# Two layers of linear attention and MLP on one core: the order of a pair's seven products, and the slots of the work beside them

## The chip, the core and the metric

The kernel runs on one core of a Trainium2 chip. The metric is the device time of one execution in microseconds (us), from launch to end; the profile also has a span, from the first to the last instruction, which is a little shorter. A core has five engines that run side by side and wait for one another by semaphores: TensorE (PE in the profile; PEld is its loading of weights) multiplies matrices, VectorE (DVE) and ScalarE (ACT) do elementwise work, GpSimd (POOL) too, and SyncE (SP) issues nearly all transfers (DMA). Each engine takes its own instructions strictly in the order in which the program issues them.

## The reference

The input x has 2048 rows (tokens) of 448 float32 numbers. Two layers with the same weights follow one another; each adds linear attention and then an MLP:

```python
phi = lambda t: jnp.where(t > 0, t + 1, jnp.exp(t)) + 1e-6
# attention, 16 heads of 28
q, k, v = split(x @ wqkv)
kv, z = einsum("bhsd,bhse->bhde", phi(k), v), einsum("bhsd->bhd", phi(k))
o = (phi(q) @ kv) / (phi(q) @ z + 1e-6)
return o @ wo
# MLP, 448 -> 1792 -> 448
return gelu(x @ w1 + b1) @ w2 + b2
# the whole
for _ in range(2):
    x = x + A(layernorm(x))
    x = x + B(layernorm(x))
```

## The kernel before

All matrix operands are kept as two numbers, a rounded high part and the rest as a low part, and a product of two such matrices is made as three: high by high, high by low, low by high. Splitting an operand therefore takes a copy on ACT (the high part) and a subtraction on DVE or POOL (the low part), and PE waits for both.

The 2048 tokens are 16 tiles of 128 rows. A layer has these stages:

**Phase 1** (`phase1`, line 797; steps by the strings `STEPS` and `STEP`) goes over the tiles: LayerNorm (`stage_a`, statistics, line 521; `stage_n`, normalising, line 524), turning the tile for PE (`stage_t`, `turn`), splitting it (`stage_x`, line 551, with the DVE subtraction of line 365), the products for k and q (psk and psq, line 382), phi, the low part of phi(k) (kl, line 611), and the sum G of phi(k) by x (`stage_g`, line 724). The turning goes by way of memory: DVE transposes blocks of 32, SP stores the square (`store_sq`) and loads it back spread (`spread`).

**Attention of the first query group and the end of phase 1** is an order written out by hand, the string `ORDER` (line 733), one token for each step. Its token `pre` loads the four phi(q) tiles of the second group (`load_pq`, lines 938 to 941) and starts the loading of a piece of w1 (`make`, line 484, with `raw`, lines 419 and 420, for the transfer).

**The MLP** treats four groups of 512 tokens. For groups 0 and 1, `classic` (line 1320) runs 14 steps each: `mlp1` multiplies by one chunk of w1 (11 matmuls of 512 columns, line 1199) and applies gelu, `mlp2` multiplies the previous chunk's gelu output by a chunk of w2 (12 matmuls of 448 columns, lines 1229 to 1231) into four accumulators. Beside them, step i does what string i of `PLAN` (line 1247) lists for the attention of groups 1 to 3: `z` and `p` (denominators, scaling, turning of phi(q): lines 951 and 962 to 973 and `turn`), `sq` and `lq` (store and load of the turned squares), `q` (splitting, ql on line 365), `o` (product with the output matrix, lines 1021 to 1025, and LayerNorm statistics), `n` (normalising), `sx`, `lx`, `x` (the same for the MLP's input). The first digit of a token is the group, the second the tile in it.

For groups 2 and 3 together, `eight` (line 1376) makes the first product by seven products instead of eight (a Strassen scheme over two chunks of w1 and the two groups) for each of seven pairs k of chunks. Products 1, 5, 6 and 7 are six matmuls of 512 columns, products 2, 3 and 4 five (line 1141). They accumulate in three banks: X takes products 1, 6, 7 and 4, Y takes 5 and 3, Z takes 2. Between them the partial sums are saved or added (`keep`, a copy on ACT, line 1145; s1, s2 and s5 with DVE adds), gelu and the split of its result follow (`high`: gelu and high part on ACT; `low`: the low part gl on DVE, line 1176), and two of the four results are stored for group 3 (`later`). `mlp2` for group 2 takes two chunks per pair, of which 2k-1 is the previous pair's second result and 2k this pair's first. Pair 0 also holds the last two chunks of group 1, whose results leave the accumulators by four DVE adds (r, line 1234), and the last piece A22 of the input (`token_piece`, line 1108, DVE subtraction on line 1112).

The seven weight combinations of the next pair are made in ten steps by a generator (`sevens`, line 445), one of which runs at every call of `step()` or `make`: the transfer (`raw`), a split with ACT line 429 and POOL lines 430 and 431, a DVE copy on line 457 that reads what line 430 wrote, POOL differences, and so on, to the last one with ACT line 478 and DVE line 479. `beside` (line 1354) loads residual rows (`back`) and, in layer 0, loads and splits wk and wq and loads x for the next layer.

**Rest** (`rest`, line 1453) loads group 3's stored gelu outputs back, splits them (`divide`) and multiplies them by w2, 14 chunks. In layer 0 the string `REST` (line 1451) puts beside it the start of layer 1: `a` statistics, `n` normalising and turning, `s` store, `p` load, `x` splitting, `m` weights. Before it, `table(AF.Exp)` loads ACT's table for exp.

The two orders that the change replaces, in short (M is a call of `mlp2`, the numbers are products, for k of 1 and more):

```
before:  1 5 M(2k-1) 6 2 7 3 4 M(2k)
after:   1 5 2 6 M(2k-1) 3 7 M(2k) 4
```

Of the kernel before, what the change touches and what calls it, by code (L numbers as in the profile page):

```python
# [11 lines left out]
AF = mybir.ActivationFunctionType  # L12
# [10 lines left out]
def linear_attn_mlp_kernel(  # L23
# [176 lines left out]
    def table(func):  # L200

        act.activation(none, tiny, func)
# [281 lines left out]
    def make(n, steps=1):  # L484
        if n < len(ahead):
            if n not in makers:
                makers[n] = (sevens if ahead[n][1] == "x" else chunks)(n)
            for _ in range(steps):
                next(makers[n], None)
# [220 lines left out]
    def stage_g(l, t, acc, mid=lambda: None):  # L710
# [22 lines left out]
    ORDER = [  # L733
# [3 lines left out]
    ] * LAYERS  # L737
    DEFER = NT - sum(tok in ("Q", "Qa", "Qy") for tok in ORDER[0].split())

# [30 lines left out]
    def load_to(l, t):  # L770
        for u in range(loaded.get(l, 0), t + 1):
            load_x(l, u)
        loaded[l] = max(loaded.get(l, 0), t + 1)
# [23 lines left out]
    def phase1(l, tr):  # L797
        za = consts.tile([128, D], F32, name="za", tag="za")
        acc = []
        load_to(l, 4 if l == 0 else NORM[l][1][-1])  # L800
        if l == 0:
            launch(za)
            load_to(l, NORM[l][2][-1])
        for t in range(l == 0, NT):
            norm = NORM[l][t] if t < len(NORM[l]) else ()
            for tok in STEPS.get((l, t), STEP).split():
                if tok[1:].isdigit() and tok[0] in "anv":
                    {"a": stage_a, "n": stage_n, "v": stage_t}[tok[0]](l, int(tok[1:]))
                elif tok == "q1":
                    stage_qphi(1)  # L810
                elif tok == "sp":
                    for key, h in list(stored):
                        block(key)
                        spread(key, h)
                elif tok == "ld" and t + 2 < len(NORM[l]):
                    load_to(l, NORM[l][t + 2][-1])
                elif tok == "a":
                    for u in norm:
                        stage_a(l, u)
                elif tok == "n":  # L820
                    for u in norm:
                        stage_n(l, u)
                elif tok == "tu":
                    for u in norm:
                        stage_t(l, u)
                elif tok == "T" and t + 1 < NT:
                    stage_b(l, t + 1, "acc" if t == 1 else "h")
                elif tok == "X" and t + 1 < NT and (l == 0 or t + 1 >= 4):
                    stage_x(l, t + 1)
                elif tok == "K":  # L830
                    stage_k(l, t)
                elif tok == "qp":
                    stage_qphi()
                elif tok == "kp":
                    stage_kphi(l, t)
                elif tok == "kh":
                    stage_kh(l, t)
                    if l == 0:
                        begin(BG[t])
                elif tok == "kl":  # L840
                    stage_kl(l, t, za)
                elif tok == "s":
                    stage_s(l, t)
                elif tok == "G" and t >= 1:
                    acc = acc or [bank("acc", 4, f"G{c}")[:, :D] for c in range(4)]
                    stage_g(l, t - 1, acc)
                elif tok == "bg" and l == 0:
                    background(BG[t - 1])
                elif tok == "Q" and t < DEFER:
                    stage_q(l, t)  # L850
            if t == 12:
                tr.wv = stage_square(wqkv[:, 2 * D:])
            if t == 13:
                trans_load(l, tr)
        return za, acc
# [252 lines left out]
    def token_piece(l, name, h, eng=dve):  # L1108
        x = view(l, name, h)
        hi, lo = (cols(placed(l, k, name, h)) for k in range(2))  # L1110
        act.copy(hi, x)
        eng.tensor_tensor(lo, x, f(hi), op=OP.subtract)
# [91 lines left out]
    def mlp2(l, b, i, then=lambda: None):  # L1204
# [49 lines left out]
        "q12 o11 n10 p22 z23 ld30",  # L1254
        "q13 o12 n11 sx10 ld31",
        "o13 n12 lq20 p23 sq21 z30 ld32",
        "n13 lx10 sx11 p30 z31 g20 ld33",
        "x10 lq21 p31 sq30 z32 g21",
        "x11 lx11 q20 p32 z33 g22",
        "x12 x13 q21 o20 p33 sq31 g23",  # L1260
        "q22 o21 n20 lq30 g30",
        "q23 o22 n21 sx20 g31",
        "q30 o23 n22 lq31 g32 g33",
        "q31 o30 n23 sx21",
        "q32 o31 n30 r10 r11",
        "q33 o32 n31 sx30 lx21 r12 r13",
        "o33 n32 lx20 tA111 b10",
# [86 lines left out]
    def beside(l, k):  # L1354

        nonlocal st_k, st_q
        if 2 <= k < 6:
            back(l, 2, k - 2)
        if 3 <= k < 7:
            add_bias(l, 2, k - 3)  # L1360
        if k == 5:
            gb.load(l, 4)
        if l + 1 == LAYERS:
            return
        if k == 5:
            load_to(l + 1, PRE - 1)
        if k == 1:
            st_k = stage_square(wqkv[:, D:2 * D])
        if k == 2:
            split_kq("k", st_k)  # L1370
        if k == 3:
            st_q = stage_square(wqkv[:, :D])
        if k == 4:
            split_kq("q", st_q)

    def eight(l, k):

        n = first_pair(l, 2) + k
        c = Pair(l, k, n)

        def step():
            if k < NP - 1:
                make(n + 1)

        c.product(1)
        s1 = c.keep(c.X, "s1")
        if k == 0:
            mlp2(l, 1, NF - 2)
            c.product(2)
            dve.tensor_tensor(s1, s1, c.Z, op=OP.add)  # L1390
            token_piece(l, "A22", 0)
            c.high(s1, 0)
        step()
        c.product(5)
        s5 = c.keep(c.Y, "s5")
        step()
        if k:
            mlp2(l, 2, 2 * k - 1)
        c.product(6)
        s2 = c.keep(c.X, "s2")  # L1400
        make(n)
        if k == 0:
            c.low(0)
            token_piece(l, "A22", 1)
            mlp2(l, 1, NF - 1)
        if k < NP - 2:
            make(n + 2)
        step()
        if k:
            c.product(2)  # L1410
            dve.tensor_tensor(s1, s1, c.Z, op=OP.add)  # L1411
            c.high(s1, 0)
            step()
        c.product(7)
        dve.tensor_tensor(s5, c.X, s5, op=OP.add)
        if k:
            c.low(0)
        c.later(s5, 1)
        step()
        c.product(3)  # L1420
        dve.tensor_tensor(s2, s2, c.Y, op=OP.add)
        c.high(s2, 1)
        step()
        if k == 0:
            mlp2(l, 2, 0)
        c.product(4)
        c.low(1)
        c.later(c.X, 0)
        step()
        if k:  # L1430
            beside(l, k)
            mlp2(l, 2, 2 * k)
        step()

    class Came:

# [11 lines left out]

    gb = Came()

    REST = ("a0", "n0 a1", "n1", "a2 m0", "s0 n2 a3", "n3 m1", "m0", "s1 p0 a4", "n4 m0", "m1", "p1 x0", "x1 m1", "", "x2 x3")

    def rest(l):

        gb.load(l, 2)
        g = gb.x.pop(0)
        gs[0] = divide_high(g)
        mlp2(l, 2, NF - 1, lambda: divide_low(g, *gs[0]))
        for i in range(NF):
            if i + 1 < NF:  # L1460
                divide(i + 1, gb.x.pop(i + 1))
            gb.load(l)
            if 5 <= i < 9:
                back(l, 3, i - 5)
            if 8 <= i < 12:
                add_bias(l, 3, i - 8)
            if l + 1 < LAYERS:
                for tok in REST[i].split():
                    t = int(tok[1:])
                    if tok[0] == "a":  # L1470
                        stage_a(l + 1, t)
                    elif tok[0] == "n":
                        stage_n(l + 1, t)
                        turn(xns[l + 1, t], ("a", l + 1, t // 4), t % 4)
                    elif tok[0] == "s":
                        store_sq(("a", l + 1, 0), t)
                    elif tok[0] == "p":
                        stage_sp(l + 1, t * 2 + 1)
                    elif tok[0] == "x":
                        stage_x(l + 1, t)  # L1480
                    elif tok[0] == "m":
                        make(first_pair(l + 1, 0) + t)
            mlp2(l, 3, i)
        gb.n = 0
# [29 lines left out]
    for l in range(LAYERS):  # L1514
# [37 lines left out]
            classic(l, b, tr)  # L1552
        for k in range(NP):
            eight(l, k)
        if l + 1 < LAYERS:
            table(AF.Exp)
        rest(l)


# [26 lines left out]
```

## Time and profile before

| | us |
|---|---|
| median of 3 runs | 864.94 |
| lowest and highest of them | 862.77, 865.45 |
| the profiled execution, its own time | 862.32 |
| its span, first to last instruction | 860.7 |
| around the span in that execution | 1.6 |

PE is busy for 847.2 us of the span (98%), DVE 616.9, ACT 442.9, POOL 392.1. The granted clock of TensorE is 1.000 over the span.

How to read the rows that follow. A row of the timeline has the start in us from the span's start, the duration in us, engine, line of the kernel, operation, what is written and read, the shape, and how many instructions it merges; in brackets stands the idle time of the engine just before it and what ended that. A row of the waits has who waited for whom, the total in us, how often and the longest. A row of a window has, for each engine, the busy us and in brackets the number of instructions, then the granted clock, the share of the DMA engines and GB/s. A row of a group has count, busy us, mean ns of one, and idle time before. Matmuls are pipelined, so that a row's duration is longer than the distance to the next row.

### The profile page before, as it was taken

To read this page: it belongs to the slowest core of one execution; us is meant where nothing else is said; L and a number is where in the kernel's file an instruction comes from. 1 tells how busy PE (TensorE), PEld (TensorE's weight loads), DVE (VectorE), ACT (ScalarE), POOL (GpSimd) and SP (SyncE) were. 2 spreads that over 40 slices of the span, in tenths; PEclk is the share of its full clock that TensorE was granted. 3 is DMA by queue.
4 is the path that set the end of the run, shared out by engine and by line. 5 is a ranking of instruction groups with operands and counts; after the bars stand their busy time and mean duration, and the time that the engine had idled before them with its cause. 6 is when DMAs were issued, how large, how long until landed. Compare 5 with 4: busy or idle time off the path is not lost.

```text
span 860.7 us, 12463 instructions
## 1 busy us (share of the span) xinstructions
PE 847.2 (98%) x4085; PEld 753.4 (88%) x4085; DVE 616.9 (72%) x1094; ACT 442.9 (51%) x883; POOL 392.1 (46%) x460
## 2 busy tenths in 40 slices
PE   9999999999999999999999999999999999999998
PEld 8899988788888888888899998988888888788897
DVE  7899586799965765465879876868998657534343
ACT  7667665335334556574345665553343346556531
POOL 3456523547426744751633344144563367453320
PEclk9999999999999999999999999999999999999999
DMA  5375736758656033418635542476668540432271
GB/s 171 119 246 178 245 104 219 256 164 278 215 193 225 13 120 114 148 60 290 213 119 190 166 158 97 130 244 213 212 209 271 194 165 3 134 101 91 98 232 43
DMA packets 103636, 142.91 MB, mean 166 GB/s; under 512 B 9876, under 2 KB 90644, under 8 KB 103572
## 3 DMA queue, kind: packets, MB, share of 16 engines
q1 hardware_dynamic: 101156, 138.77, 49.1%
q10 hardware_dynamic: 2416, 3.36, 1.2%
q8 instruction: 32, 0.52, 0.3%
q14 instruction: 32, 0.26, 0.1%
HBM read 88.94 MB, written 49.02 MB: 160 GB/s over the span
## 4 chain that ended last, share of the span: by engine, by line
PE 67%; DVE 15%; DMA 5%; issue 5%; ACT 4%; POOL 3%; SPq 0%; ACTq 0%; DVEq 0%; POOLq 0%
PE hp L1199 7%; PE G L724 7%; PE psk L382 7%; PE y L1231 7%; PE psq L382 6%; PE y L1229 6%; PE y L1230 6%; PE hx L1141 6%; PE hy L1141 3%; DVE gl L1176 2%; DVE ql L365 2%; DMA pq<-pq_d 1%; DVE pq L973 1%; DMA sp<-sq_m 1%; PE hz L1141 1%
## 5 line engine op out<-in xcount | busy, mean ns | idle before, releaser
L1229 PE MATMUL y<-w2h,gh 128*128 128x448 f32 x447 | 162.6, 364 | 1.9 <-DVE r L1234 1.7
L1230 PE MATMUL y<-w2l,gh 128*128 128x448 f32 x447 | 163.6, 366 | 0.0
L1231 PE MATMUL y<-w2h,gl 128*128 128x448 f32 x447 | 161.2, 361 | 1.8 <-DVE gl L1176 1.8
L1176 DVE TENSOR_TENSOR gl<-g,gh 128x512 fp32r<-128x512 f32 x84 | 67.4, 802 | 89.3 <-ACT gh L1172 89.3
L1199 PE MATMUL hp<-XH,W 128*128 128x512 f32 x392 | 123.6, 389 | 0.9 <-POOL W L431 0.9
L1201 ACT ACTIVATE g<-hp,b1s 128x512 f32<-128x512 f32 x56 | 38.5, 688 | 150.6 <-PE hp L1199 150.0
L213 POOL TENSOR_TENSOR brs<-bve,few 128x1 f32<-128x1 f32 x55 | 36.0, 654 | 134.3 <-DVE bve L212 130.5
L1229 PEld LDWEIGHTS y<-w2h,gh 128*128 128x128 f32 x447 | 83.7, 187 | 12.4 <-DVE r L1234 2.8
L1231 PEld LDWEIGHTS y<-w2h,gl 128*128 128x128 f32 x447 | 84.0, 188 | 10.0 <-DVE gl L1176 4.7
L1230 PEld LDWEIGHTS y<-w2l,gh 128*128 128x128 f32 x447 | 83.9, 188 | 6.2
L1199 PEld LDWEIGHTS hp<-XH,W 128*128 128x128 f32 x392 | 73.6, 188 | 13.8 <-POOL W L431 1.3
L1199 PE MATMUL hp<-XL,W 128*128 128x512 f32 x224 | 85.2, 389 | 0.0
L382 PE MATMUL psk<-wk,XH 128*128 128x448 f32 x210 | 61.8, 364 | 0.0
L563 POOL TENSOR_TENSOR xnl<-x,xnh 128x384 fp32r<-128x384 f32 x32 | 35.8, 1120 | 56.6 <-ACT xnh L562 27.8
L382 PE MATMUL psq<-wq,XH 128*128 128x448 f32 x196 | 57.2, 366 | 0.3 <-DVE eq L401 0.3
L1153 ACT ACTIVATE g<-s,b1s 128x256 f32<-128x256 f32 x84 | 38.2, 502 | 36.6 <-DVE s L1411 15.9
L1172 ACT CAST gh<-g 128x512 fp32r<-128x512 f32 x84 | 52.2, 621 | 2.7
L425 POOL TENSOR_TENSOR W<-temp,W 128x256 fp32r<-128x256 f32 x56 | 47.0, 860 | 7.6 <-ACT W L424 7.6
L1199 PEld LDWEIGHTS hp<-XL,W 128*128 128x128 f32 x224 | 42.0, 188 | 8.8
L951 POOL TENSOR_TENSOR pz<-pq,zb 128x448 f32<-128x448 f32 x24 | 28.7, 1194 | 40.6 <-DVE dn L962 17.3
L724 PE MATMUL G<-kh,xnh 128*128 128x448 f32 x128 | 46.6, 367 | 0.0
L724 PE MATMUL G<-kl,xnh 128*128 128x448 f32 x128 | 46.1, 366 | 0.0
(250 smaller groups left out, 2062.1 us busy)
## 6 DMA issues: line engine op xcount, KB each, us to landing
temp<-in_B_w_dram SPq DMA_DIRECT2D x28, 384.0 KB
x<-in_A_x_dram SPq DMA_DIRECT2D x32, 224.0 KB
pq_d<-eq SPq DMA_DIRECT2D x32, 224.0 KB
pq<-pq_d SPq DMA_DIRECT2D x32, 224.0 KB
g_d<-g SPq DMA_DIRECT2D x28, 256.0 KB
gb<-g_d SPq DMA_DIRECT2D x28, 256.0 KB
x<-x_d SPq DMA_DIRECT2D x32, 224.0 KB
sq_a<-sq SPq DMA_DIRECT2D x13, 512.0 KB
```

Of the source, the lines that this page charges most:

```text
L382: pe.matmul(o, x, p, start=(i == 0), stop=(i == 10))
L425: pool.tensor_tensor(lo, x, f(hi), op=OP.subtract)
L724: pe.matmul(acc[c], w, k, start=first and c not in others[0], stop=last and c not in others[1])
L1141: pe.matmul(o, w, r, start=(k in (1, 5, 2) and i == 0), stop=(i == len(made) - 1), skip_group_check=True)
L1153: act.activation(g[:, s].rearrange("p (u i n) -> p i u n", u=2, i=4), x[:, s].rearrange("p (i u n) -> p i u n", u=2, i=4), AF.Gelu_apprx_t ...
L1172: act.copy(gh, g)
L1176: dve.tensor_sub(gl, g, f(gh))
L1199: pe.matmul(hp, w, r, start=(k == 0), stop=(k == len(made) - 1))
L1201: act.activation(g, hp, AF.Gelu_apprx_tanh, bias=b1s[:, i:i + 1])
L1229: pe.matmul(acc[j], gh[:, s], hi, start=first, stop=False)
L1230: pe.matmul(acc[j], gh[:, s], lo, start=False, stop=False)
L1231: pe.matmul(acc[j], gl[:, s], hi, start=False, stop=stop)
```

## The change

The change moves work between places in the order of issue. The matrix products, the splits and the transfers are the same ones as before.

1. **Pairs** (`eight`). For k of 1 and more the products go 1 5 2 6 3 7 4, with chunk 2k-1 of w2 after product 6 and chunk 2k after product 7. The subtraction for gl of the first result (`low(0)`) stands after chunk 2k-1, that of the second (`low(1)`) after product 7, and `beside` after product 7. For pair 0 the order of products and chunks stays; the second half of A22 moves from before the last chunk of group 1 to after product 7, the transfer for pair 2 to before product 5, and the second result's `low(1)` to right behind its `high`.
2. **Classic** (`PLAN`). Of group 3, the tokens `p30`, `p31`, `p32` and `z31`, `z32`, `z33` go one step later, `p33` from step 12 to step 14; the store `sq30` goes from step 10 to 11, `sq31` from 12 to 14, and the load `lq31` from 15 to 16.
3. **`pre`** in `ORDER` stands earlier, right after `sa3`, the load of the last turned square of group 0's MLP input; the steps of the last phi(q) tiles and the splits `x0` to `x3`, which stood before it, now follow it.
4. **Start of layer 1**. The first two x tiles load in pair 4 instead of 5; their LayerNorm statistics run in the last pair instead of `rest`; the splits of tiles 2 and 3 run in phase 1 of layer 1 instead of `rest`; the exp table loads in the third step of `rest` instead of before it; the other tokens of `REST` shift.

```diff
-        ... sp2 Qj Qm Qe sa3 Qj Qa Qm x1 x0 Qe Qa Qm Qj x2 x3 Qe Qj Qs pre Qa Qi Qj Qs "
+        ... sp2 Qj Qm Qe sa3 pre Qj Qa Qm x1 x0 Qe Qa Qm Qj x2 x3 Qe Qj Qs Qa Qi Qj Qs "
...
-                elif tok == "X" and t + 1 < NT and (l == 0 or t + 1 >= 4):
+                elif tok == "X" and t + 1 < NT and (l == 0 or t >= 1):
...
-        "n13 lx10 sx11 p30 z31 g20 ld33",
-        "x10 lq21 p31 sq30 z32 g21",
-        "x11 lx11 q20 p32 z33 g22",
-        "x12 x13 q21 o20 p33 sq31 g23",
+        "n13 lx10 sx11 g20 ld33",
+        "x10 lq21 p30 z31 g21",
+        "x11 lx11 q20 p31 sq30 z32 g22",
+        "x12 x13 q21 o20 p32 z33 g23",
         "q22 o21 n20 lq30 g30",
-        "q23 o22 n21 sx20 g31",
-        "q30 o23 n22 lq31 g32 g33",
-        "q31 o30 n23 sx21",
+        "q23 o22 p33 n21 sq31 sx20 g31",
+        "q30 o23 n22 g32 g33",
+        "q31 lq31 o30 n23 sx21",
...
-        if k == 5:
-            load_to(l + 1, PRE - 1)
+        if k >= 4:
+            load_to(l + 1, 1 if k == 4 else PRE - 1)
...
+        onward = k == NP - 1 and l + 1 < LAYERS
...
         c.product(1)
         s1 = c.keep(c.X, "s1")
-        if k == 0:
+        if k:
+            step()
+            c.product(5)
+            s5 = c.keep(c.Y, "s5")
+            step()
+            if onward:
+                stage_a(l + 1, 0)
+            c.product(2)
+            dve.tensor_tensor(s1, s1, c.Z, op=OP.add)
+            c.high(s1, 0)
+            step()
+            c.product(6)
+            s2 = c.keep(c.X, "s2")
+            make(n)
+            if k < NP - 2:
+                make(n + 2)
+            step()
+            mlp2(l, 2, 2 * k - 1)
+            c.low(0)
+            step()
+            c.product(3)
+            dve.tensor_tensor(s2, s2, c.Y, op=OP.add)
+            c.high(s2, 1)
+            step()
+            c.product(7)
+            dve.tensor_tensor(s5, c.X, s5, op=OP.add)
+            c.low(1)
+            c.later(s5, 1)
+            step()
+            beside(l, k)
+            if onward:
+                stage_a(l + 1, 1)
+        else:
             mlp2(l, 1, NF - 2)
             c.product(2)
             dve.tensor_tensor(s1, s1, c.Z, op=OP.add)
             token_piece(l, "A22", 0)
             c.high(s1, 0)
...
+            make(n + 2)
+            step()
+            c.product(5)
+            s5 = c.keep(c.Y, "s5")
+            step()
+            c.product(6)
+            s2 = c.keep(c.X, "s2")
             c.low(0)
+            mlp2(l, 1, NF - 1)
+            step()
+            c.product(7)
+            dve.tensor_tensor(s5, c.X, s5, op=OP.add)
+            c.later(s5, 1)
             token_piece(l, "A22", 1)
+            make(n)
             step()
...
+            c.product(3)
+            dve.tensor_tensor(s2, s2, c.Y, op=OP.add)
+            c.high(s2, 1)
+            c.low(1)
+            step()
+        mlp2(l, 2, 2 * k)
+        c.product(4)
+        c.later(c.X, 0)
         step()
...
-    REST = ("a0", "n0 a1", "n1", "a2 m0", "s0 n2 a3", "n3 m1", "m0", "s1 p0 a4", "n4 m0", "m1", "p1 x0", "x1 m1", "", "x2 x3")
+    REST = ("", "n0", "n1", "a2 m0", "s0 n2", "a3 m1", "n3", "p0 m0", "s1 a4 m0", "n4", "m1", "p1 x0", "x1 m1", "")
...
             if l + 1 < LAYERS:
+                if i == 2:
+                    table(AF.Exp)
...
-        if l + 1 < LAYERS:
-            table(AF.Exp)
         rest(l)
```

More of the change, by code (lines that the diff above doesn't have):

```diff
@@ L1392, in eight @@
             c.high(s1, 0)
[L1393 to L1402, printed above, removed]
-            c.low(0)
-            token_piece(l, "A22", 1)
[L1405 to L1412, printed above, removed]
-            step()
[L1414 to L1422, printed above, removed]
+            make(n + 2)
[5 more added lines that the diff above has]
+            s2 = c.keep(c.X, "s2")
+            c.low(0)
+            mlp2(l, 1, NF - 1)
[3 more added lines that the diff above has]
+            c.later(s5, 1)
+            token_piece(l, "A22", 1)
+            make(n)
+            step()
+            c.product(3)
[6 more added lines that the diff above has]
+        c.later(c.X, 0)
         step()
         if k == 0:
[L1425 to L1433, printed above, removed]
+            step()
     class Came:
```

2 rows, old and new, of the table ORDER are left out of this document.

## The prediction

> **What bounds the kernel now.** I read the page first, then the list of whom PE waits for, then the timeline of PE around each wait, then the other engines' timelines behind it.
>
> ```profile
> span 860.7 us, 12463 instructions
> PE 847.2 (98%) x4085; PEld 753.4 (88%) x4085; DVE 616.9 (72%) x1094; ACT 442.9 (51%) x883; POOL 392.1 (46%) x460
> ```
>
> ```profile
> PE op L1023 <- DVE ql L365: 3.0, 3, 1.3
> PE y L1231 <- DVE gl L1176: 1.8, 5, 0.5
> PE y L1229 <- DVE r L1234: 1.7, 2, 0.8
> ```
>
> PE is the bound: 860.7 - 847.2 = 13.5 us of its span is idle. The change neither adds nor removes a matmul, so all that it can win is waits, and all that it can lose is new ones. The list says that the waits inside the body are almost all for DVE: three for ql (the attention of groups 1 to 3), five for gl, two for r. What one wait really costs is more than its bracket:
>
> ```profile
> 163.66 0.50 PE L1199 MATMUL hp<-XH,W 128*128 128x512 f32 x1 [0.85 <-POOL W L431]
> 164.00 0.40 PE L1199 MATMUL hp<-XL,W 128*128 128x512 f32 x1
> 164.23 0.39 PE L1199 MATMUL hp<-XH,W 128*128 128x512 f32 x1
> ```
>
> ```profile
> 164.90 0.37 PE L1022 MATMUL op<-wq,qh 128*128 128x448 f32 x1
> 165.77 0.47 PE L1023 MATMUL op<-wq,ql 128*128 128x448 f32 x1 [0.51 <-DVE ql L365]
> 166.08 0.36 PE L1021 MATMUL op<-wq,qh 128*128 128x448 f32 x1
> 166.28 0.36 PE L1022 MATMUL op<-wq,qh 128*128 128x448 f32 x1
> ```
>
> Undisturbed matmuls of 448 columns start 0.20 us apart (166.08 to 166.28), those of 512 columns 0.23 (164.00 to 164.23). Around the second wait the starts are 0.87 and 0.31 apart instead, so it lost 0.67 + 0.11 = 0.78 us where the bracket says 0.51. I add 0.27 to every bracket.
>
> **The change part by part.** The terms are PE waits, so each ends on the path.
>
> *A, `pre` earlier.* The two waits above cost 0.85 + 0.27 and 0.78: 1.9 us, in layer 0 only. Behind them stand late weights:
>
> ```profile
> 138.42 0.38 SPq L419 DMA_DIRECT2D temp<-in_B_w_dram  x1
> ```
>
> ```profile
> 144.51 0.71 ACT L424 CAST W<-temp 128x256 fp32r<-128x256 f32 x2 [3.88 <-DMA temp<-in_B_w_dram]
> ```
>
> SP issues the weight transfer of `pre` only at 138.42, behind phi(q) stores that wait for DVE, and ACT then stands 3.88 us for it, with gelu and all later weight splits queued behind. `pre` moved ahead of these stores removes that wait. ACT's later stops for transfers stay, so I take 1.4 of 1.9 (bounds 0 and 1.9). The stores behind `pre` on SP wait for six more issues; phi(q) of those tiles is read back many steps later, which hides it.
>
> *B, group 3's turning later.* The first of these rows is in step 12, the other pair in front of the next group's first chunk:
>
> ```profile
> 210.36 0.47 PE L1023 MATMUL op<-wq,ql 128*128 128x448 f32 x1 [1.20 <-DVE ql L365]
> ```
>
> ```profile
> 226.31 0.36 PE L1025 MATMUL op<-wq,ql 128*128 128x448 f32 x1
> 226.78 0.47 PE L1229 MATMUL y<-w2h,gh 128*128 128x448 f32 x1
> ```
>
> ```profile
> 203.43 0.61 DVE L962 TENSOR_REDUCE dn<-pz 128x16 f32<-128x448 f32 x1
> ```
>
> ```profile
> 206.62 0.38 DVE L310 STREAM_TRANSPOSE sq<-pq 128x128 f32<-128x128 f32 x1
> ```
>
> The ql waits of both layers: 3.0 - 0.51 = 2.49 in brackets, plus 2 x 0.27 = 3.0 us. At 226.78 the start is 0.27 late, and 0.11 follows: 0.4, which I take for layer 1 too, as it runs the same plan: 3.8 us in all. One `p` token occupies DVE from 203.43 to 207.00, 3.6 us for six instructions. Up to step 13 DVE has one `p` less to do, and the wait of 1.5 us and that of 0.4 together are less than 3.6. I take 3.5 (bounds 0 and 3.8). The `p` moved to step 14 meets this:
>
> ```profile
> 229.30:236.40 7.10, 7.10 (x35) 6.38 (x34) 5.95 (x12) 2.35 (x4) 3.96 (x5) 1.00 0.81 259
> ```
>
> DVE is free for 1.15 of 7.1 us there; the rest of the 3.6 runs into the following steps, where PE needs gl and ql one step later. On SP the store of that square stands ahead of `sx20`, a load of x and later weights, whose users are a step or more away.
>
> *C, pair 0.* The first chunk of group 2 waits for the accumulators:
>
> ```profile
> 310.23 0.47 PE L1229 MATMUL y<-w2h,gh 128*128 128x448 f32 x1 [0.83 <-DVE r L1234]
> ```
>
> ```profile
> 308.41 1.23 DVE L1112 TENSOR_TENSOR XL<-sp,A 128x512 fp32r<-128x512 f32 x1
> 309.56 2.20 DVE L1234 TENSOR_TENSOR r<-y,r 128x448 f32<-128x448 f32 x4
> ```
>
> The list has two such waits, 1.7 us, one per layer: 1.7 + 2 x 0.27 = 2.2. The adds start right when the A22 subtraction ends. Moved behind product 7, it frees 1.23 us, more than 0.83; I take 2.0 (bounds 0 and 2.2). But now product 4 needs that piece. Its chain is add, gelu, copy, subtraction, the same sequence that takes from 322.97 to 326.60 below, 3.6 us; its cover is product 3 (5 x 0.23), a chunk (12 x 0.20) and product 4's first two matmuls: 4.0. Margin 0.4; new cost 0 to 0.8 in each layer, I take 0.3, so 0.6.
>
> *D, pairs 1 to 6.*
>
> ```profile
> 326.60 0.47 PE L1231 MATMUL y<-w2h,gl 128*128 128x448 f32 x1 [0.45 <-DVE gl L1176]
> ```
>
> ```profile
> 312.21 0.41 SPq L419 DMA_DIRECT2D raw<-in_B_w_dram  x1
> ```
>
> ```profile
> 319.55 0.62 ACT L429 CAST W<-raw 128x512 fp32r<-128x512 f32 x1 [2.77 <-DMA raw<-in_B_w_dram]
> ```
>
> ```profile
> 321.91 0.29 DVE L457 COPY raw<-W 128x256 f32<-128x256 f32 x1 [5.49 <-POOL W L430]
> ```
>
> ```profile
> 322.97 0.69 DVE L1411 TENSOR_TENSOR s<-s,hz 128x512 f32<-128x512 f32 x1
> ```
>
> The weights of pair 2 are issued at 312.21, behind the stores of group 1's results; ACT, POOL and DVE's line 457 wait in turn, s1's add follows late, then gl. After the change they are issued before product 5, ahead of those stores, and gl has product 6, chunk 2k-1, and products 3 and 7 as cover instead of 7, 3 and 4. The bracket at 326.60 costs 0.72; of the five gl waits two are in `rest` (below), and the other two make 1.8 - 0.45 - 0.68 = 0.67, of which I count 0.45 + 0.27 for layer 1's pair. 1.4 (bounds 0 and 1.7). `beside` and the two statistics moved into the last pair find no weight steps left there.
>
> *E, `rest` of layer 0.*
>
> ```profile
> 415.80 0.47 PE L1231 MATMUL y<-w2h,gl 128*128 128x448 f32 x1 [0.22 <-DVE gl L1176]
> ```
>
> ```profile
> 418.93 0.48 PE L1231 MATMUL y<-w2h,gl 128*128 128x448 f32 x1 [0.46 <-DVE gl L1176]
> ```
>
> ```profile
> 397.46 1.28 ACT L202 ACT_TABLE_LOAD   x1
> ```
>
> Two waits, 0.49 + 0.73 = 1.2: gl stands on DVE behind statistics and normalising of one step. Two of five statistics and two of four splits leave; I take 1.1. The table stands ahead of the first `rest` chunk's high part; in the third step it finds ACT idle. Gain between 0 and 1.28; 0.5.
>
> *F, what is added.* The splits of tiles 2 and 3 move into phase 1 of layer 1, between DVE work that G waits for:
>
> ```profile
> 448.26 0.62 DVE L611 SCALAR_TENSOR_TENSOR kl<-psk,kh 128x448 fp32r<-128x448 f32 x1
> ```
>
> ```profile
> 448.94 0.47 PE L724 MATMUL G<-kl,xnh 128*128 128x448 f32 x1
> ```
>
> ```profile
> L365 DVE TENSOR_TENSOR XL<-sp,XH 128x512 fp32r<-128x512 f32 x42 | 36.9, 892 | 1.6 <-ACT XH L364 1.5
> ```
>
> ```profile
> L563 POOL TENSOR_TENSOR xnl<-x,xnh 128x384 fp32r<-128x384 f32 x32 | 35.8, 1120 | 56.6 <-ACT xnh L562 27.8 <-PE psk L382 27.7 <-PE y L1230 1.1
> ```
>
> kl ends at 448.88, and the matmul that reads it starts at 448.94: no margin. A split (mean 0.89) ahead of kl makes G late by about as much. I take 0.9; bounds 0, if DVE gets there earlier, and 2.0, two splits or one that waits a whole POOL subtraction (0.89 + 1.12). The Trainium skill, SBUF — State Buffer, Who interferes with whom, says that a DVE instruction with two SBUF inputs and a GpSimd one that reads SBUF exclude each other, the later waiting for the whole of the other. By it F is 2.0 and the sum 1.1 less; the 1.23 of row 308.41 against the mean of 0.89 speaks for some of that, not for all.
>
> *Sum.* Gains 1.4 + 3.5 + 2.0 + 1.4 + 1.6 = 9.9; costs 0.6 + 0.9 = 1.5; net 8.4 us. The profiled execution took 862.3 (span 860.7 and 1.6 around it) and would take 853.9. The median of the runs shown is 864.9, 2.6 above it; 8.4 off that is 856.5.
>
> **The rivals.**
>
> *R1: DVE is the bound of the attention steps.* For the windows from 163.5 to 226.8:
>
> ```profile
> sum 63.30, PE 61.33 PEld 53.83 DVE 61.29 ACT 25.33 POOL 38.85; mean PE 6.13 PEld 5.38 DVE 6.13 ACT 2.53 POOL 3.89
> ```
>
> DVE is busy 61.3 of 63.3 us. If its backlog only travels with the moved `p`, B's waits reappear after step 14: B is 0, time 856.5 + 3.5 = 860.0. For it: DVE's 97%. Against: the 1.15 us free in step 14, and more than a step of distance to the users. If several terms are only half won, the result is about the same (860 to 862). Together 0.12.
>
> *R2: the earlier `pre` collides with the loads that the MLP's first matmul waits for.*
>
> ```profile
> pq<-pq_d SPq DMA_DIRECT2D x32, 224.0 KB
> ```
>
> ```profile
> temp<-in_B_w_dram SPq DMA_DIRECT2D x28, 384.0 KB
> ```
>
> It issues 4 x 224 + 384 = 1280 KB directly behind the last turned square. If they share its bandwidth, the first matmul waits for them too: 1.31 MB at the 259 GB/s of row 229.30 is 5.1 us, in each layer. Time 856.5 + 1.4 + 10.1 = 868, slower. It decides if the square's load lasts longer than now. Against: that load is issued first on the same queue. The Trainium skill, DMA: Bandwidth & Descriptors, Issuing engines are not separate DMA queues, has all transfers interleave on the same 16 engines, which speaks for R2. Chance 0.05.
>
> *R3: line 457 now stands close in front of s1's add.* In each of the 12 pairs after a pair 0 it waits for POOL's line 430.
>
> ```profile
> 342.37 0.62 PE L1141 MATMUL hx<-XH,W 128*128 128x512 f32 x2
> ```
>
> ```profile
> 347.71 0.73 POOL L430 TENSOR_TENSOR W<-raw,W 64x256 fp32r<-64x256 f32 x1
> ```
>
> Product 2 ends 17 x 0.23 = 3.9 us into the pair; from there to the matmul that reads gl lie 17 x 0.23 + 12 x 0.20 + 0.4 = 6.7 us, and the chain needs 3.6, so s1's add may be 3.1 late. Pair 3's line 430 began 5.3 in, which puts the add at 6.4, 2.5 late. Only weights over 0.6 us later than this one cost anything; at 2 us in every pair it is 24 us and 880, slower. Chance 0.04.
>
> **How the numbers follow.** Forecast 0.79, R1 0.12, R2 0.05, R3 0.04. The bounds add up to a net of 12 at best and 5 where A or B fails in part, so 852.5 to 860; with R1 the range is 852 to 861.5, which leaves out R2, R3 and a little of both ends. A measurement of this kernel can tell 0.3%, 2.6 us, from no change: faster 0.84 (nearly all of the forecast and half of R1), same 0.07, slower 0.09.
>
> **What would show it.** Right: no ql wait in step 12; no r wait ahead of group 2's first chunk; no gl wait in pairs 1 to 6 or in `rest`; no ACT stop for the transfer of `pre`; one new wait of about 0.9 at the second G of layer 1, small ones at product 4 of pair 0. Wrong: idle PE over 6 us left in the body, or a first MLP matmul that starts later after the last psq.

## The result and the profile after

| | before | after |
|---|---|---|
| median, us | 864.39 (862.77 to 865.45, 4 runs) | 858.02 (857.30 to 859.25, 4 runs) |
| ratio, 95% interval | | 0.9929 (0.9909 to 0.9950) |
| profiled execution, its span | 862.32, 860.7 | 859.25, 857.2 |

The change makes the kernel faster by 0.7%; the forecast of 856.5 is 1.5 us below what was measured. The two profiled executions lie closer together than the medians: that of before is faster than each of the four timed runs, that of after is the slowest of its four. So I compare their waits, not their spans. As in the prediction, a wait costs its bracket and about 0.27 us.

The list of whom PE waits for, after (total us, times, longest):

```profile
PE op L1023 <- DVE ql L365: 4.1, 4, 1.7
PE warm L171 <- DVE one L165: 1.1, 1, 1.1
PE y L1229 <- DVE x L1234: 1.0, 2, 0.5
PE hp L1199 <- DVE XL L365: 0.7, 1, 0.7
PE psq L382 <- DVE eq L401: 0.2, 1, 0.2
PE G L724 <- DVE kl L611: 0.2, 1, 0.2
```

All gl and r waits are gone, as C, D and E said. But the ql waits have not gone: they went from 3.0 us in three to 4.1 in four. B has failed, A half. The timeline of PE shows the new and the grown ones, in the order of time:

```profile
136.29 1.20 PE L1199 MATMUL hp<-XL,W 128*128 128x512 f32 x4 [0.68 <-DVE XL L365]
...
210.44 0.48 PE L1023 MATMUL op<-wq,ql 128*128 128x448 f32 x1 [1.71 <-DVE ql L365]
...
227.27 0.47 PE L1229 MATMUL y<-w2h,gh 128*128 128x448 f32 x1 [0.52 <-DVE x L1234]
...
445.88 0.47 PE L724 MATMUL G<-kl,xnh 128*128 128x448 f32 x1 [0.19 <-DVE kl L611]
```

136.29 is in the first chunk of the MLP, where before there was no wait. 210.44 is the wait in step 12 that B was to remove: 1.71 instead of 1.20. 227.27 is the first chunk of w2 for group 1; its start stood 0.27 late before (226.78) and is 0.68 late now. 445.88 is the second G of layer 1, as F said (0.46 late by the distance of the starts).

Where C and D came from, on SP, ACT and DVE around pair 0 (after):

```profile
302.89 0.38 SPq L419 DMA_DIRECT2D raw<-in_B_w_dram  x1
...
306.41 2.20 DVE L1234 TENSOR_TENSOR r<-y,r 128x448 f32<-128x448 f32 x4
...
316.44 0.64 ACT L429 CAST W<-raw 128x512 fp32r<-128x512 f32 x1
...
317.98 0.29 DVE L457 COPY raw<-W 128x256 f32<-128x256 f32 x1 [1.53 <-POOL W L430]
```

Pair 2's weights are issued at 302.89 instead of 312.21, ACT no longer stands for them, and DVE's line 457 ends its wait 3.9 us earlier. The four r adds, no longer behind the A22 subtraction, start at 306.41 instead of 309.56, and product 4 of pair 0 waits nowhere (0.6 had been set aside for it).

Why B brought nothing, on DVE (after):

```profile
197.91 0.37 DVE L310 STREAM_TRANSPOSE sq<-xm 128x128 f32<-128x128 f32 x1
199.95 0.69 DVE L1176 TENSOR_TENSOR gl<-g,gh 128x512 fp32r<-128x512 f32 x1 [1.66 <-ACT gh L1172]
202.89 0.69 DVE L365 TENSOR_TENSOR XL<-sp,XH 128x512 fp32r<-128x512 f32 x1 [2.25 <-ACT XH L364]
203.50 0.61 DVE L962 TENSOR_REDUCE dn<-pz 128x16 f32<-128x448 f32 x1
```

The 3.6 us that p30 left free are spent idle: 1.66 + 2.25 = 3.9. The low part of x10 (line 365) starts at 202.89, and before it started at 202.82: it waits for ACT's high part, and that waits for a transfer. First `after`, then the kernel before:

```profile
202.24 0.62 ACT L364 CAST XH<-sp 128x512 fp32r<-128x512 f32 x1 [2.32 <-DMA sp<-sq_m]
```

```profile
202.17 0.62 ACT L364 CAST XH<-sp 128x512 fp32r<-128x512 f32 x1 [1.81 <-DMA sp<-sq_m]
202.82 0.69 DVE L365 TENSOR_TENSOR XL<-sp,XH 128x512 fp32r<-128x512 f32 x1
```

Behind it comes a `p` (203.50), as before, but now it is p30 instead of p31, and then gl and the low part of x11 up to ql. So ql ends at 210.38, before it ended at 210.31. PE gets there 0.4 us earlier than before, since other waits are gone, and stands longer.

### The profile page after: what moved, and what is told of

Read it like the earlier page. It is cut to its first block, busy times and chain, and to the rows that moved or that the text cites. A ratio compares the mean times of both kernels' runs of the same rounds, so it can differ in the third digit from the quotient of the medians.

```text
span 857.2 us, 12480 instructions
## 1 busy us (share of the span) xinstructions
PE 846.2 (99%) x4085; PEld 755.0 (88%) x4085; DVE 621.9 (73%) x1094; ACT 443.1 (52%) x883; POOL 393.1 (46%) x460
## 4 chain that ended last, share of the span: by engine, by line
PE 75%; DVE 11%; DMA 5%; issue 4%; ACT 2%; POOL 2%; ACTq 0%; SPq 0%; DVEq 0%; POOLq 0%
PE hp L1199 9%; PE hx L1141 9%; PE y L1230 8%; PE y L1229 8%; PE y L1231 8%; PE G L724 7%; PE psk L382 6%; PE psq L382 5%; PE hy L1141 4%; PE hz L1141 2%; DVE ql L365 1%; DMA sp<-sq_m 1%; DMA wq<-Ml 1%; DMA temp<-in_B_w_dram 1%; DVE pq L973 1%
## 5 line engine op out<-in xcount | busy, mean ns | idle before, releaser
L213 POOL TENSOR_TENSOR brs<-bve,few 128x1 f32<-128x1 f32 x55 | 33.9, 616 | 138.4 <-DVE bve L212 133.0
```

## The experiments

Ratios are to the kernel before, with their 95% interval. The first four kernels ran on one chip, the next four on another, the last four on a third, each time beside the kernel before.

**plan_before**: `after` with the string PLAN of the kernel before.

```diff
-        "n13 lx10 sx11 g20 ld33",
-        "x10 lq21 p30 z31 g21",
+        "n13 lx10 sx11 p30 z31 g20 ld33",
+        "x10 lq21 p31 sq30 z32 g21",
...
```

> The changed kernel with the PLAN of the kernel before (part B undone, all else as changed). Theory S (the slot that B emptied cannot be used): in the changed kernel DVE stands idle from 198.28 to 202.89, because the subtraction of x10 (XL, line 365) waits for ACT's high part, and that for the transfer sp<-sq_m, which lands near 202.2 whatever DVE does; so B moved one `p` out of a slot that was free anyway, and the next `p` came to stand between that subtraction and ql. By S, putting p30 back changes nothing for PE: ql waits of 1.7 to 1.9 us in step 12 stay, span 857.2 within 0.6. The forecast as written (B is worth 3.5): span 860.7. Rival R1 (DVE simply full, its backlog travels with the `p`): also no change, so this run only separates the forecast from S and R1.

857.47 us, 0.9939 (0.9917 to 0.9960): taking B out costs nothing that can be measured. The forecast's 3.5 us are not there: the ql waits of step 12 stand in both kernels. In this trace p30 is back ahead of x10, and DVE still waits for the high part:

```profile
202.09 0.69 DVE L365 TENSOR_TENSOR XL<-sp,XH 128x512 fp32r<-128x512 f32 x1 [0.51 <-ACT XH L364]
```

**p30_back**: `after` with one token moved back.

```diff
-        "n13 lx10 sx11 g20 ld33",
-        "x10 lq21 p30 z31 g21",
+        "n13 lx10 sx11 p30 g20 ld33",
+        "x10 lq21 z31 g21",
```

> The changed kernel with one token moved: p30 goes back from step 10 into step 9, the slot that DVE now idles through; p31, p32 and p33 stay where the change put them, so step 10 has no `p`. Theory S: the 3.6 us of p30 leave the stretch between the subtraction of x10 and ql, and nothing is paid for it, as DVE was idle there. The ql waits of step 12 (starts 1.88 and 1.57 late, and 0.12 behind each) go in both layers, and the waits for the accumulators in front of group 2's first chunk (0.68 + 0.11 each) go or shrink too, since one `p` less stands ahead of them: 3.7 to 5.3 us less, span 852.0 to 853.5. Rival R1 (DVE is full from 163 to 227 and the order within it does not matter): no gain, span 857.2 within 0.6. The forecast's reasoning (each `p` in an earlier step costs what it occupies) would make it 860 or more.

853.93 us, 0.9891 (0.9870 to 0.9912); the interval does not overlap that of plan_before. The ql waits of step 12 are gone in both layers, those in front of group 1's first chunk of w2 fell to 0.28 and 0.21 late. DVE now does p30 in the slot, still waits 2.3 us in three pieces, and goes on to ql with no `p` between:

```profile
197.56 0.57 DVE L962 TENSOR_REDUCE dn<-pz 128x16 f32<-128x448 f32 x1
...
202.37 0.69 DVE L365 TENSOR_TENSOR XL<-sp,XH 128x512 fp32r<-128x512 f32 x1 [0.75 <-ACT XH L364]
204.23 0.69 DVE L1176 TENSOR_TENSOR gl<-g,gh 128x512 fp32r<-128x512 f32 x1 [1.16 <-ACT gh L1172]
205.27 0.86 DVE L365 TENSOR_TENSOR XL<-sp,XH 128x512 fp32r<-128x512 f32 x1 [0.35 <-ACT XH L364]
206.06 1.22 DVE L365 TENSOR_TENSOR ql<-sp,qh 128x512 fp32r<-128x512 f32 x1
```

ql ends at 207.28; the matmul that reads it starts undisturbed at 207.90. R1 as a mechanism (DVE full, order without effect) falls: the same work in another order is 3.5 us faster than in plan_before.

**pair0_only**: the kernel before, with only pair 0 as in the change.

```diff
         if k == 0:
             mlp2(l, 1, NF - 2)
...
+            make(n + 2)
+            step()
+            c.product(5)
...
+            token_piece(l, "A22", 1)
+            make(n)
...
```

> The kernel before with only pair 0's part of the change: the transfer for pair 2 ahead of product 5, the second half of A22 behind product 7, the second result's subtraction behind its high part. Pairs 1 to 6 keep the order 1 5 M 6 2 7 3 4 M, and everything else is as before. Theory L (late weights): the gl waits of pair 1 (starts 0.62 and 0.64 late, 0.11 behind each, and 0.3 at product 7 of layer 0) go although the order of products stays, because the transfer is issued ahead of the stores; with the r waits gone (0.99 + 0.11 in each layer) the span falls by 3.5 to 4.0, to 856.7 to 857.2. Rival O (the new order of products and chunks is what covers gl): the gl waits of pair 1 stay, the span falls by 2.2 only, to 858.5. Pair 0's new product 4 may wait up to 0.3 in each layer by the forecast.

858.59 us, 0.9948 (0.9929 to 0.9967). The r waits and the gl waits of pair 1 are gone in both layers, though pairs 1 to 6 keep the old order; only those of `rest` are left of the gl waits (0.7 us in two). Theory L holds: pair 0's part, not the order, removed D's waits. That edit has two other shifts beside the transfer, not tried apart; that it is the transfer is read from the rows. Line 457, which waited 5.49 us for late weights, waits 1.52:

```profile
301.94 0.37 SPq L419 DMA_DIRECT2D raw<-in_B_w_dram  x1
...
317.04 0.29 DVE L457 COPY raw<-W 128x256 f32<-128x256 f32 x1 [1.52 <-POOL W L430]
```

**pre_back**: `after` with `pre` in its old place.

```diff
-        ... sa3 pre Qj Qa Qm x1 x0 Qe Qa Qm Qj x2 x3 Qe Qj Qs Qa ...
+        ... sa3 Qj Qa Qm x1 x0 Qe Qa Qm Qj x2 x3 Qe Qj Qs pre Qa ...
```

> The changed kernel with `pre` back in its place of the kernel before (part A undone). In the changed kernel PE waits 0.84 + 0.11 at 136.29 for the subtraction of the MLP's input, whose two instructions take 2.24 us together instead of 1.28, beside a POOL product (line 951, 1.63 us instead of 1.16) that `pre` brought forward. Theory P (POOL work beside the subtraction): with `pre` back that wait goes, the subtraction takes 1.3 us again, and the wait at step 4 for the weights that POOL splits (1.02 + 0.11 at 163.66 before) comes back, as ACT stands for the issue of the M transfers (wq<-Mh) in both kernels and so the end of that chain does not move: span 857.2 within 0.4, the wait only changes its place. Rival (the forecast: late weights of `pre` cause the stop in step 4): the waits of 1.1 and 0.8 of step 4 are there and nothing else changes much, span 858.2 or more with the 0.95 won back at 136.29 included.

857.69 us, 0.9936 (0.9917 to 0.9956), the same as with `pre` early. The wait at 136.29 is gone, and one for POOL's weights in step 4 is back, smaller than before (0.43 + 0.11 late); so is a gl wait of layer 1 at 560 (0.31 + 0.12). The two low parts ahead of the MLP, first in `after`, then here:

```profile
134.00 2.24 DVE L365 TENSOR_TENSOR XL<-sp,XH 128x512 fp32r<-128x512 f32 x2
```

```profile
133.96 1.28 DVE L365 TENSOR_TENSOR XL<-sp,XH 128x512 fp32r<-128x512 f32 x2
```

In `after` POOL works beside them, since `pre` has brought its phi(q) there (line 951 at 134.06, 1.63 us instead of 1.16); in pre_back it has no work there. Both sides are slowed. That agrees with the Trainium skill, SBUF — State Buffer, Who interferes with whom, which has a DVE instruction with two SBUF inputs and a GpSimd one that reads SBUF exclude each other. How much it costs hangs on who starts first: in p30_back, also with `pre` early, the product begins at 133.25, before the subtraction (133.79), it takes 1.15, the two low parts 1.76, and PE's start there is 0.35 late instead of 0.83. In the traces of the eight other kernels with `pre` early, p30_back among them, that start is 0.15 to 0.38 late; the 0.83 of `after` is the most.

A later stop of ACT, on which the weights of step 4 hang, is there in both, with the same releaser; the first row is of `after`, the second of pre_back:

```profile
160.86 0.62 ACT L429 CAST W<-temp 128x512 fp32r<-128x512 f32 x1 [4.82 <-DMA wq<-Mh]
```

```profile
160.44 0.62 ACT L429 CAST W<-temp 128x512 fp32r<-128x512 f32 x1 [3.84 <-DMA wq<-Mh]
```

ACT issues fourteen transfers of M in steps 0 to 3 (line 924) and stands for them.

**order_only**: the kernel before with only the new order in pairs 1 to 6.

```diff
+        if k:
+            step()
+            c.product(5)
...
+            c.product(2)
...
+            c.product(6)
...
+            mlp2(l, 2, 2 * k - 1)
+            c.low(0)
...
```

> The kernel before with only the new order of pairs 1 to 6 (1 5 2 6 M 3 7 M 4); pair 0, with its late transfer for pair 2 and the early half of A22, is as before. Theory L (the gl waits of pair 1 came from late weights alone): DVE's line 457 still waits for POOL's weights and stands ahead of s1's add, so a wait stays in pair 1 of both layers (0.3 to 0.9), and the r waits ahead of group 2's first chunk (0.99 + 0.11 in each layer) stay: span 860.7 within 0.8. Rival O (the new order alone covers gl): no wait over 0.1 in pairs 1 to 6, span about 859.0 (1.7 less), the r waits staying.

868.24 us, 1.0062 (1.0039 to 1.0085): slower, more than either theory said. The gl wait of pair 1 is gone, but a worse one stands in its place:

```profile
322.07 0.62 ACT L429 CAST W<-raw 128x512 fp32r<-128x512 f32 x1 [2.87 <-DMA raw<-in_B_w_dram]
...
324.35 0.29 DVE L457 COPY raw<-W 128x256 f32<-128x256 f32 x1 [5.51 <-POOL W L430]
...
325.33 0.91 ACT L1153 ACTIVATE g<-s,b1s 128x256 f32<-128x256 f32 x2 [1.85 <-DVE s L1393]
326.27 0.62 ACT L1172 CAST gh<-g 128x512 fp32r<-128x512 f32 x1
326.79 0.58 ACT L1145 COPY s<-hx 128x512 f32<-128x512 f32 x1
...
327.43 0.81 PE L1141 MATMUL hx<-XH,W 128*128 128x512 f32 x2 [2.21 <-ACT s L1145]
```

The late weights hold POOL and DVE's line 457, which stands in front of s1's add (R3's place); the gelu of s1 (325.33) stands on ACT for that add, and behind it in ACT's queue the copy (326.79) that saves product 6 from bank X. Product 7 writes that bank and waits (327.43). In the old order product 6 and its copy came before product 2 and that gelu. Layer 1 has the same wait (1.80 at 756.16).

**lx10_early**: `after` with the load of x10's square one step earlier; p30 stays late.

```diff
-        "o13 n12 lq20 p23 sq21 z30 ld32",
-        "n13 lx10 sx11 g20 ld33",
+        "o13 n12 lq20 lx10 p23 sq21 z30 ld32",
+        "n13 sx11 g20 ld33",
```

> The changed kernel with the load of x10 and x11's turned square (`lx10`) moved from step 9 to step 8, ahead of the store sq21, for which it now stands in SP's queue until 196.4; p30 stays in step 10. Theory S (the slot is empty because the subtraction of x10 waits for this transfer): the load is issued near 190.8, XH is there before 200, DVE does the subtraction of x10 and p30 about 2.2 us earlier instead of idling, and the ql wait of step 12 (1.88 and 1.57, 0.12 behind each) shrinks to 0.3 or less in both layers: 3.0 to 3.8 us less, span 853.4 to 854.2. Rival: the transfer lands at the same time whenever it is issued, or something else holds ACT's high part: no change, 857.2 within 0.6.

854.11 us, 0.9897 (0.9878 to 0.9915), as theory S said. First the issue of that load (line 332) in `after`, behind the store of line 323, then here, ahead of it:

```profile
195.64 0.32 SPq L323 DMA_DIRECT2D sq_q<-sq  x1
196.40 0.88 SPq L332 DMA_DIRECT2D sp<-sq_m  x1
```

```profile
190.95 0.36 SPq L332 DMA_DIRECT2D sp<-sq_m  x1
...
195.17 0.32 SPq L323 DMA_DIRECT2D sq_q<-sq  x1
```

In the changed kernel it stands in SP's queue behind a store that waits for a `p` of group 2. Issued before that store, its high part runs at 199.35 without a wait, DVE's low part at 200.09, and the ql waits of step 12 are gone.

**m_on_sp**: p30_back, with the transfers of M issued by SP.

```diff
-                act.dma_start(f(out[at + r - lo:at + r - lo + n]), f(src[r // G][r % G:r % G + n]))
+                sp.dma_start(f(out[at + r - lo:at + r - lo + n]), f(src[r // G][r % G:r % G + n]))
```

> The kernel with p30 back in step 9 (span 850.4), and the fourteen transfers of M that ACT issues in steps 0 to 3 of the MLP in each layer (wq<-Mh, wq<-Ml, line 924) issued by SP instead. Theory M (ACT stands for these issues, its line 429 up to 4.8 us at 161, and the weights, gelu and ql of step 4 are late by that): the stop of ACT goes, and with it the ql wait of step 4 (0.65 + 0.11 and 0.67 + 0.11): 1.5 us less, span 848.9. Rival: SP stands for them in turn, and its loads of phi(q) and weights come late: waits of a microsecond or more in steps 1 to 5, span 851 or more.

851.62 us, 0.9868 (0.9848 to 0.9888). The interval overlaps that of p30_back, but the list of waits is as theory M said, with no ql wait left in either layer; its last rows:

```profile
PE psk L652 <- ACT wk L138: 0.3, 1, 0.3
PE hp L1199 <- DVE XL L365: 0.2, 1, 0.2
PE G L724 <- DVE kl L611: 0.2, 1, 0.2
```

ACT's line 429 of this place now runs at 155.17; in p30_back it ran at 160.21, behind a stop of 4.83 us.

**x23_rest**: p30_back, with the splits of tiles 2 and 3 in `rest` again.

```diff
-                elif tok == "X" and t + 1 < NT and (l == 0 or t >= 1):
+                elif tok == "X" and t + 1 < NT and (l == 0 or t + 1 >= 4):
...
-    REST = (... "p1 x0", "x1 m1", "")
+    REST = (... "p1 x0", "x1 m1", "x2 x3")
```

> The kernel with p30 back in step 9 (span 850.4), and the splits of tiles 2 and 3 of layer 1 done in the last step of `rest`, as before the change, and not in phase 1. Forecast's term F (they stand ahead of kl in phase 1): the wait of the second G (0.46 + 0.11, and 0.11 just ahead of it) goes, 0.6 to 0.7 us less: 849.8. The splits stand beside the last chunk of `rest`; forecast's term E counted two of four splits among what took the gl waits of `rest` away: if that is right, some of these waits (0.2 to 0.7) come back; if the spreading of statistics and normalising did it alone, none does.

853.28 us, 0.9892 (0.9874 to 0.9910). The wait of the second G is gone here and no gl wait comes back in `rest`, so these splits had no share in E.

**best**: the three edits together (p30_back, m_on_sp, x23_rest).

> The changed kernel with three things that the runs so far point to: p30 back in step 9, the M transfers issued by SP, the splits of tiles 2 and 3 back in the last step of `rest`. By the sum of the stalls that each took away alone: the kernel with the first two has a span of 849.1, and the wait of the second G (0.46 + 0.11, 0.11 just ahead) goes: 848.5, median 851. If the parts get in each other's way (the splits beside the last chunk of `rest`, or a later start of layer 1), 849.1 or more.

851.62 us, 0.9874 (0.9857 to 0.9890), no better than m_on_sp; its span is 850.0, not the 848.5 that the single gains add up to. The wait of the second G, gone in x23_rest, is back here at its full size, without any split ahead of kl:

```profile
442.32 0.47 PE L724 MATMUL G<-kl,xnh 128*128 128x448 f32 x1 [0.19 <-DVE kl L611]
```

So F's cause is not shown: there the chain up to kl has no margin (as at 448.94 in the kernel before), and whether PE stands 0.46 for it differs between kernels with and without the splits.

**best_pre_back**: best, with `pre` in its old place (the edit of pre_back).

> The same three-part version with `pre` back in its place of the kernel before. Theory M (ACT stood in step 4 for the M transfers, not for the weights of `pre`): with the M transfers on SP there is no wait in step 4 either way, and the wait at 135.5 (0.38 + 0.11) for the subtraction beside POOL's product goes: 0.5 us less than the three-part version. Rival (the forecast's part A: late weights of `pre` hold ACT): the waits of step 4 in layer 0 come back, 1.4 to 1.9 us more; the gl wait at 560 of layer 1 (0.31 + 0.12), which the run with `pre` back showed, comes back by either.

852.70 us, 0.9884 (0.9869 to 0.9899); not told apart from best by the times. In the trace the wait at 136 is gone, and one in step 4 is there, of 1.39 + 0.11, but not for weights:

```profile
163.36 0.62 ACT L364 CAST qh<-sp 128x512 fp32r<-128x512 f32 x1 [2.81 <-DMA sp<-sq_q]
```

ACT's stop for the weights of `pre` is back (3.51 us, up to 144.49), but from 147.50 ACT waits for PE again, so it is not that. With M's transfers and a late `pre` in one queue, SP issues the square of phi(q) at 155.14 instead of 154.41 in best (the MLP starts at the same time in both), and ACT splits it at 163.36 instead of 162.15. The gl wait of layer 1 at 559 is back as well (0.33 + 0.12). So in the traces `pre` earlier is worth something once ACT is free, by another road than the one I named.

**best_old_order**: best, with pairs 1 to 6 in the old order and pair 0 as changed.

> The three-part version with pairs 1 to 6 in the order of the kernel before (1 5 M 6 2 7 3 4 M), pair 0 with its early transfer kept. Theory L (the transfer for pair 2 is what matters; the new order alone made the kernel 0.6% slower): no wait over 0.15 in pairs 1 to 6, span within 0.7 of the three-part version. Rival O (the new order has a share in it once the weights are early): gl or keep waits of 0.2 or more return in pairs, 1 us or more in the span.

852.28 us, 0.9880 (0.9865 to 0.9895), between the theories: in layer 0 small gl waits return at the last pair (0.11 and 0.22 late, 0.11 behind each), about 0.7 us in all, none in layer 1. In this trace the new order shows a gain only at that pair, beside which LayerNorm statistics of layer 1 stand; the times do not tell it from best.

**best_rest_before**: best, with REST and the two statistics as before.

```diff
-    REST = ("", "n0", "n1", "a2 m0", "s0 n2", "a3 m1", ...
+    REST = ("a0", "n0 a1", "n1", "a2 m0", "s0 n2 a3", "n3 m1", ...
```

> The three-part version with the string REST of the kernel before and the two statistics back in it; the exp table stays in the third step. If the spreading of statistics and normalising took the gl waits of `rest` away: waits near steps 5 to 9 of `rest` in layer 0 come back (0.18 + 0.11, 0.39 + 0.11, 0.63 + 0.11), 1.5 us more, and the wait at the first chunk (0.33 + 0.11 before) stays away, as the table, which stood ahead of it, is elsewhere. If the table did it all, the span is that of the three-part version.

852.44 us, 0.9883 (0.9868 to 0.9898). Two of the three gl waits expected come back, 0.38 + 0.11 and this one of 0.60 + 0.11, and the one at the first chunk of `rest` does not:

```profile
413.06 0.47 PE L1231 MATMUL y<-w2h,gl 128*128 128x448 f32 x1 [0.43 <-DVE gl L1176]
```

So spreading statistics and normalising removed those of E, 1.2 us; the wait at the first chunk is gone by something else, of which the table's move is the likely part, not tried alone.

## Why the prediction was right, and where it was not

That the time came out right is luck: A and B fell 6.7 us short of the forecast, the other terms brought 2.2 us more than it, and 2.5 us of the difference of the medians lie in no wait that the two traces show. By the distance of the starts in the two profiles, in us:

| term | forecast | measured | |
|---|---|---|---|
| A, `pre` | +1.4 | -0.3 | wrong cause |
| B, PLAN | +3.5 | -1.5 in the trace, 0 in time | wrong |
| C, pair 0 | +2.0 - 0.6 | +2.2 | right, no new wait |
| D, pairs | +1.4 | +2.0 | right, by pair 0's part |
| E, `rest` | +1.6 | +2.1 | right, spreading shown, splits without a share |
| F, G of layer 1 | -0.9 | -0.6 | size right, cause open |
| sum | 8.4 | 3.9 | |

The measured column is the waits gone less the waits new; A has those of the first MLP steps of both layers, a gl wait gone from layer 1 (565.24, 0.43) among them. The profiled spans differ by 3.5, the medians by 6.4 (the interval is 4.3 to 7.9). What the medians hold beyond the waits is not explained; single executions of one kernel differ by up to 5 us (plan_before, 855.89 to 860.98). A part of it may be the granted clock: on the first chip the kernel before took 863.5 to 865.9 in the four runs with a mean clock of 0.998 or less and 861.6 to 863.2 in the seven others. For the four runs of the result this is not shown.

**B failed at one step**: "Up to step 13 DVE has one `p` less to do, and the wait of 1.5 us and that of 0.4 together are less than 3.6." The sum of DVE's work said nothing about when it can be done. The low part of x10 is tied to a transfer that lands near 202.2, and work taken from in front of it is not won. The trace of before had it, unread: that subtraction started at 202.82, on the end of ACT's high part (202.17 + 0.62), and ACT stood 1.81 us for the transfer; DVE showed no idle time only because p30 filled it. p30_back and lx10_early show both sides of this: put the `p` back into the slot, or make the slot shorter, and each takes the wait away. R1 gave B's right value, 0, for a wrong reason: DVE was not full but tied. The time alone could not tell R1's 860.0 from the forecast.

**A failed at its cause.** "`pre` moved ahead of these stores removes that wait" is true of the transfer that it names, but hardly of the wait: the row of 144.51 runs only 0.2 us earlier in `after`, now behind a transfer of M.

```profile
144.31 0.71 ACT L424 CAST W<-temp 128x256 fp32r<-128x256 f32 x2 [2.95 <-DMA wq<-Mh]
```

The late weights of step 4 hang on ACT, which stood up to 4.8 us for the transfers of M; "ACT's later stops for transfers stay" was priced at the 0.5 that I left out, and was nearly all of it. m_on_sp shows that they were the cause. In place of the wait at 163.66 came the one at 136.29, in the first chunk, near where R2 had looked, but at 0.95 us instead of 5.1, and not for bandwidth: POOL's work slowed the subtraction there. With the 0.26 to 0.49 (0.15 to 0.38 and 0.11 behind it) of the other kernels in its place, A would be a gain of 0.1 to 0.3, still far from 1.4. In layer 1 a ql wait at step 4 is new (0.68 + 0.11); it is there in pre_back and plan_before too, so neither `pre` nor PLAN brought it, and not in m_on_sp beyond 0.10.

**C and D** were right in mechanism and a little small. D's reason, late weights, is borne out by pair0_only and the rows shown with it; the new order was not needed for it. What D and E brought beyond the forecast are late starts that the list of waits does not name, as at 324.32 and 410.51. The clause that the new order gives gl a longer cover is true, but without the earlier transfer it makes the kernel slower (order_only), by R3's chain with one more link. R3's chance was given to the whole change; what keeps it away is pair 0's part, by the rows the earlier call of `make`.

**Of what was to be seen**: right were the r waits, the gl waits and the new wait at G; ACT's stop for the transfer of `pre` went, and a stop for M took its place. Wrong were the ql wait of step 12 and the small waits at product 4; and the sign given for failure, idle PE over 6 us in the body, was there: the list above sums to 6.2 without PE's first wait at the start.

## What to carry to other kernels

Before moving work off a full engine, find the instructions in the stretch that start right on another engine's or a transfer's end: work in front of such a point is free to stay as long as it fits the gap, work behind it delays everyone. Follow a wait to the end of its chain, past engines that only stood in a queue, and price that end; a stop that is noted and set aside can be where the gain goes. And when a change has two parts in one place, try each alone: here the one with the small diff carried the gain, and the one with the large diff cost 0.6% by itself.

## What the runs showed of the hardware

A stop of PE can cost more than its length. In the trace of order_only two waits, of 1.87 and 2.21 us, were each followed by 4 us with a mean granted clock of 0.57 (third column from the end), with matmuls of 448 columns 0.37 us apart instead of 0.20:

```profile
211.50:215.50 4.00, 3.88 (x11) 3.44 (x12) 3.86 (x8) 0.93 (x2) 3.29 (x3) 0.57 0.84 278
215.50:219.00 3.50, 3.50 (x18) 3.11 (x18) 3.40 (x9) 1.35 (x4) 0.00 (x0) 1.00 0.18 65
324.00:327.40 3.40, 1.22 (x6) 0.67 (x4) 0.89 (x2) 2.04 (x5) 3.17 (x5) 1.00 0.12 41
327.40:331.40 4.00, 3.98 (x11) 3.30 (x12) 3.76 (x5) 1.37 (x4) 2.07 (x3) 0.57 0.00 1
```

Waits of 1.71 (after, 210.44) and 1.80 us (order_only, 756.16) left the clock at 1.00. Four us at 0.57 lose 1.7 us. So in these traces a wait of about 2 us was where it began to count nearly twice; with two cases on either side the point is not sharp. Nor is it the same in every execution: two of the six runs of order_only had a mean clock of 0.999 and took 866.0 and 866.2 us, the four others 0.995 to 0.997 and 867.6 to 871.2. The Trainium skill, TensorE: Matmul & The Clock Gate, Part 1, puts the fall to half rate at an idle window of about 3.4 us; the trace of order_only shows it after less, and the measurement decides.
